# Half of the up product by Strassen's method in a fused retention and feed-forward kernel

## The chip, the cores and the metric

The kernel runs on one core of one Trainium2 chip. The metric is device microseconds (us) of one execution. Four compute engines work side by side, each strictly in the order of its own instructions: PE (matrix products, with its weight loads), DVE (VectorE), ACT (ScalarE) and POOL (GpSimd). SP issues most of the transfers. Engines wait for each other through semaphores.

## The reference

```python
scores = scale * np.matmul(q, k.transpose(0, 1, 3, 2))          # B=8 batches, H=8 heads, S=576, D=64
Dmat = np.where(rel >= 0, gamma[:, None, None] ** rel[None, :, :], 0.0)
ret = scores * Dmat[None, :, :, :]
attn = np.matmul(ret, v)
x = np.ascontiguousarray(attn.transpose(0, 2, 1, 3)).reshape(B * S, H * D)   # 4608 x 512
h = x @ w_in                                                     # 512 x 2048
g = h * np.clip(h + 3.0, 0.0, 6.0) / 6.0
out = g @ w_out                                                  # 2048 x 512
```

A decayed attention (retention) feeds a two-layer network. Its first product, `x @ w_in`, is the up product; the second, `g @ w_out`, is the down product.

## The kernel before

The 4608 tokens are taken in nine blocks of 512 (`NB = 9`). Block 0 holds the first 64 tokens of each batch, the other eight the remaining 512 of one batch each. Retention is worked in chunks of 128 tokens, four to a block, with a state carried from chunk to chunk.

Work is staged so that PE always has three kinds of it at hand. In stage `kb` of the last loop (L811 to L839) PE does the down product of block `kb`, the up product of block `kb+1`, and the retention of block `kb+2`. The order is written out by hand: `tc.manual_schedule` keeps each engine's instructions in the order in which the program issues them.

- **The up product** comes in 16 units per block (`up_steps`, L491). A unit is 128 rows of `h` by 512 tokens: four products over the four 128-row pieces of `d_model`. `product` (L149) splits each into two matmuls of 64 output rows. The result lies in a PSUM bank `ph`. ACT reads it, `u = relu(ph/6 + 0.5)` (L510); DVE finishes the gate, `g = min(u, 1) * ph` in fp16 (L512). `u` has three buffers.
- **The down product** from block 2 on is by Strassen's method (`down_strassen`, L562): seven products of 16 steps, 112 steps per block, each step two matmuls of 256 columns. I write D for a step. Its results lie in two banks `st`. ACT takes p1, p5, c11, c12 and u2 out of them (L595 to L631), DVE u3 and c21, and POOL adds in SBUF. The sums of quarters of `g` that it needs (s1 to s4, L517) are made on DVE by `side_sums` (L525), one at each "+" of the order.
- **Retention**, in letters of the order: c casts a chunk to fp16 (k on ACT, L188; q and v on POOL, L192 and L195), a scores, x and i the two halves of the output (`po`, copied to `xT` by ACT, L369), s the states, u the addition to the running state (DVE L313 and L316, then POOL L317), z its cast on ACT (L323 to L326).

The table `STEADY` (L710) gives after which unit each letter comes; `per = 7` puts seven D between two units. All PSUM tiles but those of the down product share six banks (tag "pp"), which are handed on in order. A unit that starts takes the bank that was taken six tiles earlier, once its last reader is done.

Of the kernel before, what the change touches and what calls it, by code (L numbers as in the profile page):

```python
# [21 lines left out]
def kernel(  # L22
# [9 lines left out]
    nc = tc.nc  # L32
# [3 lines left out]
    P = 128  # L36
# [39 lines left out]
    warm = const.tile([P, 1], FP32)  # L76
    mask = const.tile([P, P], FP16)
    SUB = P // 2
    query = const.tile([P, P], FP32)
    early = io.tile([P, H, D], FP32, tag="fv", name="early").rearrange("p h d -> p (h d)")  # L80
    dist, far = early[:, 0:P], early[:, P:2 * P]
# [5 lines left out]
    zh = [const.tile([P, NP, D], FP32, name=f"zh{b}") for b in range(B)]  # L87

    def indices():
        nc.vector.memset(half, 0.5)  # L90
# [58 lines left out]
    def product(out, lhs, rhs, **flags):  # L149

        for h2 in range(2):
            r = slice(h2 * D, h2 * D + D)
            nc.tensor.matmul(out[r], lhs[:, r], rhs, skip_group_check=True, **flags)  # L153
# [219 lines left out]


    def idle_products(n):
        idle = psum.tile([P, NP, P], FP32, tag="pp", name="idle")
        for _ in range(n):
            product(idle, ident16, ident16.unsqueeze(1).to_broadcast([P, NP, P]), start=True, stop=True)


    hd = {}
# [105 lines left out]
    def up_unit(kb, u, th=None):  # L487
        for _ in up_steps(kb, u, th):
            pass
# [39 lines left out]
    def store(kb, m2, o, m=slice(0, 2), cols=slice(0, DM)):  # L529
# [3 lines left out]
        else:  # L533
            rows = out.rearrange("(e m s) n -> e s m n", e=2, s=S)
            for e in range(2):
                nc.sync.dma_start(rows[e, 0:TL, 2 * m2:2 * m2 + 2, :], o[TL * e:TL * e + TL])

    def out_tile(kb, m2):
        return work.tile([P, 2, DM], FP32, tag=f"o{m2}", bufs=2, name=f"o{m2}_{kb}")

    kept = deque()


    def down_plain(kb):
# [139 lines left out]
    def do(todo):  # L684
        for what, c in todo:
            if what == "+":
                side_sums(c)
            elif c < NCH:
                {"c": cast, "t": lambda c: transposes(c, True, "kq" if c < PE_T else "k" if c < PE_K else ""), "a": scores, "s": states, "u": add, "z": past,
                 "x": cross_over, "i": inner, "k": keys_heads, "h": head_states, "o": lambda _: store(*kept.popleft())}[what](c)  # L690

    def go(plan, kb=None, down=None):
# [3 lines left out]
        for item in plan.split():  # L696
# [13 lines left out]
    STEADY = {0: [("u", 1)], 1: [("z", 1), ("+", 1)], 2: [("+", 1)], 4: [("c", 4)],  # L710
# [4 lines left out]

    FIRST_STEADY = {0: [("+", 1), ("c", 3)], 1: [("D", 7), ("a", 0), ("s", 0), ("u", 0)],
# [5 lines left out]

    with tc.manual_schedule(engines={ENG.PE, ENG.DVE, ENG.Pool, ENG.Activation, ENG.SP}):
        sp, act, pool = nc.sync, nc.scalar, nc.gpsimd
        on_act, on_dve = nc.scalar.copy, nc.vector.tensor_copy
        indices()
        for nm in ("k", "q"):
            landed = load_half(0, nm, 0, sp)
            keys = landed if nm == "k" else keys
            load_half(0, nm, 1, act)  # L730
        nc.scalar.activation(warm, half, ACTF.Exp)
        load_half(1, "q", 0, sp)
        load_half(1, "q", 1, act)
        for i in (2, 3):
            for e in range(2):
                load_half(i, "q", e, sp, keys)
        for i in (1, 2, 3):
            for e in range(2):
                load_half(i, "k", e, pool, None if i == 1 else keys)
            if i == 1:  # L740
                nc.gpsimd.memset(pick, 0.0)  # L741
        for i in range(NP):
            load_values(i)
        win_piece(0, 2)
        for n in (1, 2, 3):
            win_piece(n)
        wout = [wout_piece(pc) for pc in (0, 2, 1, 3)]
        distances()
        idle_products(5)
# [5 lines left out]
        idle_products(4)  # L755
# [9 lines left out]
        idle_products(1)  # L765
# [4 lines left out]
        idle_products(1)  # L770
# [37 lines left out]
        go("U1 D3 t14 U1 D2 U1 U1 D2 x13 a14 s14 i13 u14 z14 o1 c16 U1 D2 U1 D2 t15 U1 D2 U1 D2 +1 U1 x14 a15 s15 i14 u15 z15 "  # L808
           "c17 D2 U1 D2 +1 U1 D2 +1 U1 D2 x15 +1 U1 i15 t16 c18 +1 U1 D2 t17 U1 U1",
           2, down)  # L810
        for kb in range(2, NB):  # L811
            for _ in down:
                pass
            plain = kb < FIRST
            down = down_plain(kb) if plain else down_strassen(kb)
            per = 4 if plain else 7
            table = FIRST_STEADY if kb == 2 else STEADY
            c = NCB * (kb + 2)
            owed = 0
            for u in range(NFC):  # L820
                if u == 0:
                    owed += per - 2
                    for _ in range(per - 2):
# [5 lines left out]
                owed -= per  # L829
                while owed < 0:  # L830
                    next(down, None)
                    owed += 1
                for w, i in table.get(u, []):
                    if w == "D":
                        for _ in range(i):
                            next(down, None)
                        owed += i
                    else:
                        do([(w, i if w == "+" else c + i)])  # L839
        for _ in down:  # L840
            pass
# [30 lines left out]
```

## Time and profile before

| | |
|---|---|
| median of three runs | 300.67 us (300.67 to 300.8) |
| the profiled execution | 301.02 us, of which the profile's span is 299.3 us |
| PE busy | 287.4 us, 96% of the span |
| DVE, ACT, POOL busy | 216.2, 193.9, 133.7 us |
| stages kb = 2 to 7 in the span | 109.8 to 281 us, about 29 us each, the last 26 |
| clock of PE granted | 1.00 in every stretch |

A line of the timeline gives the start from the span's beginning, the time to the end, engine, line, operation, output and inputs, and how many instructions are merged. A bracket at its end gives idle time before it and what ended that. A line of the groups gives line, engine, operation, shapes and count, then busy time and the mean of one in ns, then idle time ahead of them. A line of the table by stretch gives, for each engine in the order PE, PEld (its weight loads), DVE, ACT and POOL, the busy time and the number of instructions.

### The profile page before, as it was taken

How to read it: one execution, taken by the hardware profiler on the slowest of the kernel's cores; microseconds unless marked ns; L12 is line 12 of the kernel's file. 1: busy time of each engine (PE TensorE's matmuls, PEld its weight loads, DVE VectorE, ACT ScalarE, POOL GpSimd, SP SyncE). 2: the span in 40 equal slices, each digit the busy share in tenths (PEclk: the TensorE clock that was granted, in tenths of full speed). 3: DMA queues.
4: the chain of work that ended last, by engine and by line, in shares of the span. 5: the costliest groups of instructions: out<-in, count | busy, mean ns of one | idle time of the engine just before them, and what ended most of it. 6: DMA issues, size and time to landing. Idle time of an engine off the chain costs nothing.

```text
span 299.3 us, 12661 instructions
## 1 busy us (share of the span) xinstructions
PE 287.4 (96%) x5574; PEld 219.3 (73%) x5574; DVE 216.2 (72%) x388; ACT 193.9 (65%) x360; POOL 133.7 (45%) x170
## 2 busy tenths in 40 slices
PE   4999998999999999999999999999999999999995
PEld 2776644777556667888777878778778987778894
DVE  7749545669897778788967797688869776647654
ACT  3748854799866696686677577667766574565420
POOL 8971057526762920719631962386247003100510
PEclk9999999999999999999999999999999999999999
DMA  6999999998999999997999999999906100200114
GB/s 157 157 182 213 186 227 209 227 228 183 161 216 164 249 202 191 178 239 195 225 220 225 169 201 216 150 177 247 148 3 142 72 2 30 102 15 2 72 72 140
DMA packets 119542, 47.86 MB, mean 160 GB/s; under 512 B 92352, under 2 KB 114880, under 8 KB 119488
## 3 DMA queue, kind: packets, MB, share of 16 engines
q1 hardware_dynamic: 114336, 41.56, 71.1%
q0 software_dynamic: 4720, 5.11, 10.5%
q8 instruction: 43, 0.70, 1.0%
q10 hardware_dynamic: 432, 0.39, 0.5%
q14 instruction: 11, 0.09, 0.1%
HBM read 36.70 MB, written 9.44 MB: 154 GB/s over the span
## 4 chain that ended last, share of the span: by engine, by line
PE 79%; DMA 9%; POOL 6%; SPq 2%; ACT 2%; issue 1%; DVE 1%; POOLq 0%; ACTq 0%
PE ph L153 37%; PE pm L153 29%; DMA wout<-in_moe_w_out_dram 6%; PE pd L153 5%; PE po L231 4%; DMA fq<-in_q_dram 2%; PE pa L231 2%; SPq L174 2%; POOL hv L439 1%; POOL hk L399 1%; POOL win L658 1%; PE pu L231 1%; POOL ws L741 1%; PE ptk L153 1%; POOL q L192 1%
## 5 line engine op out<-in xcount | busy, mean ns | idle before, releaser
L153 PE MATMUL ph<-xT,win 128*64 128x512 f16 (+1 forms) x1248 | 144.8, 364 | 1.2 <-DMA win<-in_moe_w_in_dram 0.5
L512 DVE SCALAR_TENSOR_TENSOR g<-u,ph 128x512 f16<-128x512 f32 (+1 forms) x156 | 98.8, 643 | 53.1 <-ACT u L510 52.6
L510 ACT ACTIVATE u<-ph,half 128x512 f32<-128x512 f32 (+1 forms) x156 | 100.5, 659 | 43.0 <-PE ph L153 40.6
L153 PEld LDWEIGHTS <-win 128*64 128x64 f16 x1248 | 82.9, 136 | 28.6 <-DMA win<-in_moe_w_in_dram 1.1
L153 PEld LDWEIGHTS <-g 128*64 128x64 f16 x928 | 51.1, 110 | 14.9 <-issue 0.4
L153 PEld LDWEIGHTS <-s 128*64 128x64 f16 x896 | 50.3, 110 | 8.1 <-issue 0.2
L317 POOL TENSOR_TENSOR z<-z,gpow 128x256 f32<-128x256 f32 x24 | 15.8, 657 | 69.1 <-DVE z L316 51.2
L153 PE MATMUL pm<-ws,s 128*64 128x256 f16 x672 | 45.6, 273 | 0.0
L192 POOL TENSOR_TENSOR q<-fq,dec 128x512 f16<-128x512 f32 x32 | 36.7, 1166 | 3.4 <-DVE zh L282 1.7
L369 ACT CAST xT<-po 128x256 f16<-128x256 f32 (+1 forms) x44 | 22.5, 583 | 23.4 <-PE po L231 22.5
L195 POOL TENSOR_TENSOR v<-fv,dec 128x512 f16<-128x512 f32 x32 | 35.4, 1111 | 2.1 <-DMA fv<-in_v_dram 2.1
L591 POOL TENSOR_TENSOR u<-u,p 128x512 f32<-128x512 f32 x7 | 8.9, 1271 | 60.4 <-ACT u L631 54.2
L153 PE MATMUL pd<-wout,g 128*64 128x512 f16 x256 | 34.7, 382 | 0.1
L153 PE MATMUL pm<-wout,g 128*64 128x256 f16 x448 | 31.1, 273 | 0.0
L266 DVE TENSOR_TENSOR a<-pa,mask 128x256 f16<-128x256 f32 (+1 forms) x44 | 21.9, 539 | 8.4 <-PE pa L231 4.7
L188 ACT CAST k<-fk 128x512 f16<-128x512 f32 x32 | 19.9, 622 | 2.1 <-DMA fk<-in_k_dram 2.1
L527 DVE TENSOR_TENSOR s<-g 128x1024 f16<-128x1024 f16 x28 | 19.3, 692 | 0.2
L323 ACT CAST z<-z 128x512 f16<-128x512 f32 x24 | 14.9, 622 | 5.1 <-DVE z L313 4.7
L153 PE MATMUL pm<-ws,g 128*64 128x256 f16 x224 | 16.7, 274 | 0.0
L153 PE MATMUL pm<-wout,s 128*64 128x256 f16 x224 | 16.3, 273 | 0.1
L527 DVE TENSOR_TENSOR s<-g,s 128x1024 f16<-128x1024 f16 x14 | 13.3, 949 | 0.0
L231 PE MATMUL po<-qT,z 64*64 64x64 f16 x512 | 12.5, 198 | 0.4 <-ACT z L326 0.3
(106 smaller groups left out, 270.0 us busy)
## 6 DMA issues: line engine op xcount, KB each, us to landing
fk<-in_k_dram SPq DMA_DIRECT2D x32, 256.0 KB, 4.6
fq<-in_q_dram SPq DMA_DIRECT2D x16, 512.0 KB, 6.0
fv<-in_v_dram SPq DMA_DIRECT2D x32, 256.0 KB, 5.5
out_dram<-o SPq DMA_DIRECT2D x14, 512.0 KB, 3.8
wout<-in_moe_w_out_dram POOLq DMA_DIRECT2D x4, 512.0 KB, 17.9
out_dram<-o SPq DMA_DIRECT2D x7, 256.0 KB, 5.4
win<-in_moe_w_in_dram POOLq DMA_DIRECT2D x3, 512.0 KB, 10.9
hq<-in_q_dram SPq DMA_DIRECT2D x6, 128.0 KB, 4.6
```

What stands on the lines that cost most here:

```text
L153: nc.tensor.matmul(out[r], lhs[:, r], rhs, skip_group_check=True, **flags)
L188: nc.scalar.copy(by_head(k16), in_rows(st[c]["fk"]))
L192: nc.gpsimd.tensor_tensor(by_head(q16[:, e]), in_rows(st[c]["fq"][:, :, e, :]), in_rows(dd[:, 2 + e, 0:H, :]), ALU.mult)
L195: nc.gpsimd.tensor_tensor(v16, st[c]["fv"], dd[:, 1, H:2 * H, :], ALU.mult)
L231: return lambda: nc.tensor.matmul(*args, skip_group_check=True, **flags)
L266: nc.vector.tensor_tensor(a16[:, a, 0:n].rearrange("p x i q -> p (x i) q"), pa[a].rearrange("p x i q -> p (x i) q"), m, ALU.mult)
L317: nc.gpsimd.tensor_tensor(new, new, decay, ALU.mult)
L323: nc.scalar.copy(z16, zs[c])
L369: nc.scalar.copy(xt[:, s], po[s].rearrange("p x n (e r) -> p x n e r", e=2))
L510: nc.scalar.activation(uu[:, 0:n], ph[:, 0:n], ACTF.Relu, bias=half, scale=1.0 / 6.0)
L512: nc.vector.scalar_tensor_tensor(out=g[:, hf, ths, jr, :], in0=by_half(uu), scalar=1.0, in1=by_half(ph), op0=ALU.min, op1=ALU.mult)
L527: nc.vector.tensor_tensor(*pend.popleft())
```

## The change

Stages 3 to 7 no longer follow `STEADY` but a new order, `PLAN`. In it eight of the 16 units, those of the first half of `d_ff`, are replaced by two groups of four, `up_quad`, called Q (its first part) and q (each later part). A group computes its 512 rows by 512 tokens in seven products of half the size instead of eight. Each of the seven is four product steps of 256 columns, which add up in three banks x, z and y. Partial results p and q are copied by ACT to SBUF, added by DVE or POOL, and gated as before. One of the four gates of a group is done by POOL in two instructions (`min`, then a product), the others by DVE.

The order inside a group, with names used later: x1 and z (product steps on PE), copy pa (ACT, bank x), z+=p (DVE); y1, copy q (ACT, bank y), gate z, x2, copy pb (ACT, bank x); y2, y+=p (DVE); x3, copy pc (ACT, bank x), gate y, q+=p (POOL); gate q (POOL); x4, gate x.

The method needs sums of quarters of `w_in` (made once by POOL, W) and of x (made for each block by two instructions on DVE, t1 and t2, and two on POOL, t3 and t4, at T). They take the room of tiles that are no longer used; the output tiles go from two buffers to one. At the start, idle products that keep PE occupied are 80 columns wide instead of 512, with more of them.

```diff
+    def sums_of_w(jq):
+        w, (s1, s2, s3, s4) = w_of(jq), [w_sums[jq][:, n] for n in range(4)]
+        a11, a12, a21, a22 = [w[:, 2 * k:2 * k + 2, JP * i:JP * i + JP] for i in range(2) for k in range(2)]
+        for o, x, y, op in ((s1, a21, a22, ALU.add), (s2, s1, a11, ALU.subtract), (s3, a11, a21, ALU.subtract),
+                            (s4, a12, s2, ALU.subtract)):
+            for c in range(2):
+                nc.gpsimd.tensor_tensor(o[:, c], x[:, c], y[:, c], op)
+    def sums_of_x(kb):
+        b11, b12, b21, b22 = [xts[kb][:, 2 * k:2 * k + 2, HB * t:HB * t + HB] for k in range(2) for t in range(2)]
+        t1, t2, t3, t4 = [x_sums[:, n] for n in range(4)]
+        nc.vector.tensor_tensor(t1, b12, b11, ALU.subtract)
+        nc.vector.tensor_tensor(t2, b22, t1, ALU.subtract)
+        nc.gpsimd.tensor_tensor(t3, b22, b12, ALU.subtract)
+        nc.gpsimd.tensor_tensor(t4, b21, t2, ALU.subtract)
+    def gate(kb, g, src, eng):
+        u = work.tile([P, BLK], FP32, tag="u", bufs=3, name=f"u{kb}")
+        u = u.rearrange("p (j t) -> p j t", j=JP)
+        nc.scalar.activation(u, src, ACTF.Relu, bias=half, scale=1.0 / 6.0)
+        if eng is nc.vector:
+            eng.scalar_tensor_tensor(out=g, in0=u, scalar=1.0, in1=src, op0=ALU.min, op1=ALU.mult)
+        else:
+            eng.tensor_scalar(u, u, 1.0, None, ALU.min)
+            eng.tensor_tensor(g, u, src, ALU.mult)
+    def up_quad(kb, jq):
...
+        def one(n, lhs, rhs, more=False):
+            for j in range(JP):
+                for c in range(2):
+                    product(b[n][:, j, :], lhs(c, j), rhs(c), start=(c == 0 and j == 0 and not more), stop=(c == 1))
+        b["x"] = bank("x")
+        one("x", plain(0, 0), x(0, 0))
+        nc.scalar.copy(p, b["x"])
+        b["z"] = bank("z")
+        one("z", plain(0, 1), x(1, 0))
+        nc.vector.tensor_tensor(b["z"], b["z"], p, ALU.add)
+        yield
+        b["y"] = bank("y")
+        one("y", summed(1), xs(1))
+        nc.scalar.copy(q, b["y"])
+        gate(kb, g[:, 0, 0:JP], b["z"], nc.vector)
+        one("x", summed(2), xs(2), True)
+        nc.scalar.copy(p, b["x"])
+        yield
+        one("y", summed(4), x(1, 1), True)
+        nc.vector.tensor_tensor(b["y"], b["y"], p, ALU.add)
+        yield
+        one("x", summed(3), xs(3), True)
+        nc.scalar.copy(p, b["x"])
+        gate(kb, g[:, 1, 0:JP], b["y"], nc.vector)
+        nc.gpsimd.tensor_tensor(q, q, p, ALU.add)
+        yield
+        gate(kb, g[:, 1, JP:JQ], q, nc.gpsimd)
+        yield
+        one("x", plain(1, 1), xs(4), True)
+        gate(kb, g[:, 0, JP:JQ], b["x"], nc.vector)
+        yield
-    STEADY = {0: [("u", 1)], 1: [("z", 1), ("+", 1)], 2: [("+", 1)], 4: [("c", 4)],
...
+    PLAN = ("D5 Q0 u1 c4 D4 q z1 +1 D6 q +1 D4 q D8 q D2 q U4 D7 U5 D13 a2 x0 s2 i0 u2 "
+            "U6 u3 +1 W1 c5 U7 D7 z2 +1 Q1 c6 z3 D4 q +1 D6 q D4 q +1 D8 q D2 q U12 D9 U13 D15 a4 x2 s4 i2 u4 D1 "
+            "U14 z4 c7 +1 U15 T D7 +1")
...
+            if SIDE <= kb < NB - 1:
+                steady(kb, down)
+                continue
```

`SIDE` is 3. `steady` walks through `PLAN`; W1 acts in stage 3 alone (W0 stands in stage 2). Casts (c) and most of retention run out with the chunks: stages 3, 4 and 5 have all of it, stage 6 has one group of scores and no casts, stage 7 has neither.

More of the change, by code (lines that the diff above doesn't have):

```diff
@@ L86 @@
     gpow = const.tile([P, NP], FP32)
-    zh = [const.tile([P, NP, D], FP32, name=f"zh{b}") for b in range(B)]
+    states_of_heads = const.tile([P, B, NP, D], FP32)
+    zh = [states_of_heads[:, b] for b in range(B)]
     def indices():
@@ L375, in idle_products @@
     def idle_products(n):
-        idle = psum.tile([P, NP, P], FP32, tag="pp", name="idle")
+        idle = psum.tile([P, 80], FP32, tag="pp", name="idle")
         for _ in range(n):
-            product(idle, ident16, ident16.unsqueeze(1).to_broadcast([P, NP, P]), start=True, stop=True)
+            product(idle, ident16, ident16[:, 0:80], start=True, stop=True)
     hd = {}
@@ L536, in store @@
                 nc.sync.dma_start(rows[e, 0:TL, 2 * m2:2 * m2 + 2, :], o[TL * e:TL * e + TL])
+    late_out = [const.tile([P, 2, DM], FP32, name=f"late{m2}") for m2 in range(2)]
     def out_tile(kb, m2):
-        return work.tile([P, 2, DM], FP32, tag=f"o{m2}", bufs=2, name=f"o{m2}_{kb}")
+        return late_out[m2] if kb == 1 else work.tile([P, 2, DM], FP32, tag=f"o{m2}", bufs=1, name=f"o{m2}_{kb}")
     kept = deque()
+    SIDE = 3
+    JP = JQ // 2
+    w_sums = {0: wout16[:, 0:JH, HM:DM].rearrange("p (n c) (j x) -> p n c j x", n=4, j=JP),
+              1: late_out[1].rearrange("p m n -> p (m n)").bitcast(FP16).rearrange(
+                  "p (n c j x) -> p n c j x", n=4, c=2, j=JP)}
@@ new lines, with w_of @@
+    x_sums = late_out[0].rearrange("p m n -> p (m n)").bitcast(FP16).rearrange("p (n c t) -> p n c t", n=4, c=2)
+    part = [const.tile([P, JP, HB], FP32, name="part0"),
+            states_of_heads[:, 0:2].rearrange("p b i d -> p (b i d)").rearrange("p (j t) -> p j t", j=JP)]
+    def w_of(jq):
+        return win16[jq].rearrange("p c (x j) -> p c j x", j=JQ)
+    def sums_of_w(jq):
[5 more added lines that the diff above has]
+                nc.gpsimd.tensor_tensor(o[:, c], x[:, c], y[:, c], op)
@@ new lines, in up_quad @@
+    def up_quad(kb, jq):
+        if (kb, jq) not in gt:
+            gt[kb, jq] = [gp.tile([P, 2, 2, JQ, HB], FP16, tag="g", bufs=4, name=f"g{kb}_{jq}")]
+        g = gt[kb, jq][0][:, 0]
+        w = w_of(jq)
+        plain = lambda i, k: (lambda c, j: w[:, 2 * k + c, JP * i + j, :])
+        summed = lambda n: (lambda c, j: w_sums[jq][:, n - 1, c, j, :])
+        x = lambda k, t: (lambda c: xts[kb][:, 2 * k + c, HB * t:HB * t + HB])
+        xs = lambda n: (lambda c: x_sums[:, n - 1, c, :])
+        bank = lambda n: psum.tile([P, JP, HB], FP32, tag="pp", name=f"pq{kb}_{jq}_{n}")
+        p, q = part
+        b = {}
+        def one(n, lhs, rhs, more=False):
[29 more added lines that the diff above has]
+        yield
@@ L748 @@
         distances()
-        idle_products(5)
+        idle_products(30)
         mask_of_heads(0)
@@ L754 @@
         mask_of_heads(1)
-        idle_products(4)
+        idle_products(23)
         cast_heads(0, "q", on_dve)
@@ L764 @@
         mask_of_heads(3)
-        idle_products(1)
+        idle_products(6)
         turn_heads(2, "k", on_act)
@@ L769 @@
         scores_heads(1)
-        idle_products(1)
+        idle_products(6)
         turn_heads(3, "k", on_act)
@@ L810, with steady @@
            2, down)
+        def steady(kb, down):
+            c0 = NCB * (kb + 2)
+            u, quad = 0, None
+            for item in PLAN.split():
+                what, n = item[0], int(item[1:] or 0)
+                if what == "D":
+                    for _ in range(n):
+                        next(down, None)
+                elif what == "U":
+                    up_unit(kb + 1, n)
+                elif what == "Q":
+                    quad = up_quad(kb + 1, n)
+                    next(quad)
+                elif what == "q":
+                    next(quad)
+                elif what == "T":
+                    if kb + 2 < NB:
+                        sums_of_x(kb + 2)
+                elif what == "W":
+                    if kb == SIDE:
+                        sums_of_w(n)
+                else:
+                    do([(what, n if what == "+" else c0 + n)])
         for kb in range(2, NB):
@@ L813 @@
                 pass
[L814 to L817, printed above, removed]
+            down = down_strassen(kb)
+            if SIDE <= kb < NB - 1:
+                steady(kb, down)
+                continue
+            table = FIRST_STEADY if kb == 2 else {}
             c = NCB * (kb + 2)
@@ L821 @@
                 if u == 0:
-                    owed += per - 2
-                    for _ in range(per - 2):
+                    owed += 5
+                    for _ in range(5):
                         next(down, None)
@@ L828 @@
                     side_sums(1)
[L829 removed]
+                owed -= 7
                 while owed < 0:
@@ L837 @@
                         owed += i
+                    elif w == "W":
+                        sums_of_w(i)
+                    elif w == "T":
+                        sums_of_x(kb + 2)
                     else:
```

3 lines of the change are left out of this document (1 added, 2 removed), and 8 rows, old and new, of tables (FIRST_STEADY, STEADY).

## The prediction

> **What bounds the kernel now.** I read the busy times first, then the stages one by one, then the chain that ended last, then each engine's timeline at a stage border.
>
> ```profile
> PE 287.4 (96%) x5574; PEld 219.3 (73%) x5574; DVE 216.2 (72%) x388; ACT 193.9 (65%) x360; POOL 133.7 (45%) x170
> ```
>
> The table by stretch, for one stage (kb = 4):
>
> ```profile
> 168.00:197.20 29.20, 29.20 (x606) 23.34 (x604) 22.54 (x39) 19.83 (x35) 15.17 (x15) 1.00 1.14 184
> ```
>
> PE is busy for all of it, DVE for 22.5 us, ACT for 19.8, POOL for 15.2. The chain gives PE's pace:
>
> ```profile
> 168.11 1.73 PE ph L153 x16
> 169.84 1.31 PE pm L153 x24
> 171.15 0.86 PE ph L153 x8
> ```
>
> A unit takes 0.86 us, and 24 matmuls of 256 columns (12 D) take 1.31, so a D takes 0.109. The twelve D are the last seven of block 3 and five of block 4. So the border is at 169.84 + 7 x 0.109 = 170.60, which I call t = 0. The other engines there:
>
> ```profile
> 169.32 0.70 ACT L510 ACTIVATE u<-ph,half 128x512 f32<-128x512 f32 x1
> ...
> 171.02 0.70 ACT L510 ACTIVATE u<-ph,half 128x512 f32<-128x512 f32 x1
> ```
> ```profile
> 170.66 0.94 DVE L527 TENSOR_TENSOR s<-g,s 128x1024 f16<-128x1024 f16 x1
> 171.75 0.69 DVE L512 SCALAR_TENSOR_TENSOR g<-u,ph 128x512 f16<-128x512 f32 x1
> 172.47 0.69 DVE L527 TENSOR_TENSOR s<-g 128x1024 f16<-128x1024 f16 x1
> 173.08 0.68 DVE L591 TENSOR_TENSOR o<-pm,u 128x512 f32<-128x512 f32 x1
> 173.68 0.68 DVE L512 SCALAR_TENSOR_TENSOR g<-u,ph 128x512 f16<-128x512 f32 x1
> ```
> ```profile
> 171.01 1.49 POOL L195 TENSOR_TENSOR v<-fv,dec 128x512 f16<-128x512 f32 x1
> 175.29 0.61 POOL L317 TENSOR_TENSOR z<-z,gpow 128x256 f32<-128x256 f32 x1 [2.79 <-DVE z L316]
> 175.87 2.94 POOL L192 TENSOR_TENSOR q<-fq,dec 128x512 f16<-128x512 f32 x2
> 178.77 1.04 POOL L195 TENSOR_TENSOR v<-fv,dec 128x512 f16<-128x512 f32 x1
> ```
>
> Here is what matters: at the border DVE and ACT are behind PE. Unit 15 left PE before 169.84; its gate on DVE starts at 171.75. PE does not feel it, since six banks lie between. When an engine has work queued it starts the next instruction about 0.6 us after the last (172.47, 173.08, 173.68); a dependent one waits for the whole 0.69, then starts within 0.05.
>
> **What the change takes from PE.** Four units take 4 x 0.865 = 3.46 us. A group has seven products of four pairs of 256 columns, 7 x 4 x 0.109 = 3.03. Gain 0.43 a group, 0.86 a stage, 4.3 us over five stages. Nothing else is gained.
>
> **What it adds.** From these groups:
>
> ```profile
> L595 ACT COPY p<-pm 128x512 f32<-128x512 f32 x7 | 4.1, 579 | 2.1 <-PE pm L153 2.1
> L591 DVE TENSOR_TENSOR u<-pm,p 128x512 f32<-128x512 f32 x6 | 4.1, 685 | 0.1
> L591 POOL TENSOR_TENSOR u<-u,p 128x512 f32<-128x512 f32 x7 | 8.9, 1271 | 60.4 <-ACT u L631 54.2
> ```
>
> Per group: four copies on ACT at 0.58, one instruction more on DVE at 0.69 (two sums, one gate less), and three on POOL: q+=p at 1.27, the fp16 product between 1.04 (a quiet cast of v) and 1.49, and `min`, which the trace does not show, between 0.20 (the small L123 on 4 elements) and 1.27. I take 0.8, nearer to the 0.61 of L317, which reads as many elements. Per stage t1 and t2 take about 0.33 each on DVE (half of the 0.69 of a sum of 1024; at most 0.69), t3 and t4 1.04 each (0.61 to 1.49). By sums all have room: ACT 24.5, DVE 24.6, POOL about 24 in a stage of 28.3. But the group turns slack into **waits**: x2, x3 and x4 add into the bank that ACT has to have copied, so PE now stands behind ACT and DVE several times in one group, where before it had six banks of distance. So I follow the queues. The order and the waits are those of the changed program as built; durations and backlog are those above.
>
> **First group, t from the border.** DVE: gate of unit 15 at 1.15, t1 1.75, t2 2.10 to 2.43, s1 2.42, c21 3.03, z+=p 3.63 to 4.31 (pa has been ready since 1.75). ACT: pa 1.17 to 1.75, cast of k, q to 3.36, then gate z's relu waits for z+=p: 4.34 to 5.03, then pb to 5.5. PE without waits: D5, x1 and z, D4 to 1.84, y1, x2, D6, y2, D4, and x3 at 4.21. With them: y1 waits for t1 until 2.15 (0.31 lost), x3 would start at 4.52 and waits for pb until 5.55 (**1.03** lost). Then DVE does gate z, s2, y+=p to 7.06, ACT pc to 7.67; x4, which would start at 7.07 (x3 0.43, ten D 1.09), waits until 7.72 (**0.65**). Together 2.0 us. In stage 7 neither casts nor additions of states lie in between, and the trace of its border (unit 15's gate on DVE 0.63 after it) gives 0.8 + 0.54 = 1.34.
>
> In stages 3, 4 and 5 POOL comes late as well. Its queue is: v of a chunk to 1.9, t3, t4 to 4.0, then the state's product (waits for DVE, 5.15), two casts of q (2.94 before, 2.04 elsewhere; 2.4 taken), v, and only then, at 9.2, q+=p, for which pc was ready at 7.7. q+=p ends at 10.5. Behind it in ACT's queue stand gate q's relu, gate x, unit 8 and p5: 10.55 + 3 x 0.6 + 0.55 = 12.9. PE has the 13th D after unit 9 at 11.95 and needs p5: **1.0** lost.
>
> **Second group.** By the same walk x2 and y2 wait 0.05 and 0.45 (casts and state casts ahead of pa and q on ACT), x3 0.15, x4 0.5 (gate z, s1 and y+=p on DVE between pb and pc). Then the firmest of all. Let pc end at T. PE: x4 0.43, unit 12 0.86, eight D 0.87: at T + 2.2 it needs u2 out of its bank, for the first D of the seventh product. ACT's queue behind pc: gate y, then gate q, which waits for q+=p until T + 1.35, gate x, unit 12, u2: 1.4 + 3 x 0.6 + 0.57 = T + 3.8. **1.6** lost in each of five stages, whatever the rest. Together 2.75 with retention, 2.05 in stages 6 and 7 (x4 and u2).
>
> Stage 3 has W1 too: eight instructions on POOL (0.61 each, from L317; 0.3 to 0.75) between the state's product at 17.2 and 22.1. y2 needs the last: 1.95 more. The casts behind it push q+=p to 26.6, and u2 comes 3.65 after its D instead of 1.6; without x3's and x4's waits, 3.35 more in all.
>
> **Sum.** Lost less 0.86 gained: stages 4 and 5 2.0 + 1.0 + 2.75 - 0.86 = 4.9 each, stage 3 4.9 + 3.35 = 8.25, stage 6 2.0 + 2.05 - 0.86 = 3.2, stage 7 1.34 + 2.05 - 0.86 = 2.5. 9.8 + 8.25 + 3.2 + 2.5 = 23.7. On the profiled execution's 301.02 (span 299.3) that is 324.7; it lies 0.35 above the median of the runs, so **324.4** against 300.67.
>
> **At nothing I cost** W0 in stage 2 (POOL is busy 11.6 of 29.2 us there; without that room about 5), the single output buffers (a store lands in 3.8 us, the next use is a stage later), and the idle products: 30 of 80 columns are 2400, five of 512 are 2560, and PE waits there for casts anyway (up to 0.8 later if each took a D's 0.109).
>
> **GpSimd and VectorE.** The two casts of q took 2.94 us while DVE made sums of g from SBUF, and 2.04 at 165.69, when DVE read PSUM; DVE's sum took 0.94 beside POOL's work and 0.68 in the quiet last stages. The Trainium skill, "SBUF — State Buffer", section "SBUF: two separate sides", says that a VectorE instruction with two inputs in SBUF and a GpSimd one that reads SBUF share a port pair that one holds for its whole length. The trace agrees, and the rule speaks against this change, which adds work on both sides of it. By the rows q+=p would then take 1.27 x 2.94 / 2.04 = 1.83; that is a rival below.
>
> **Rivals.** (1) POOL is in time: the casts of q pass in the gaps, W1 goes unseen. Then only the waits between PE, ACT and DVE stay: 3.2 in each of four stages, 2.5 in the last, +15.3: 316.0. For it: POOL idles half of the time now. Against: the order of its queue. (2) POOL and DVE block each other more: 0.56 more at each q+=p, 0.25 at each DVE sum on the path, about 1.4 in three stages and 0.8 in two, +5.8: 330. For it the 0.94 and 2.94; against, that q+=p has no DVE sum beside it for most of its length. (3) **Faster.** The place is u2 behind pc. A stage gains once u2 ends within 2.2 + 0.86 = 3.1 us of pc instead of 3.8, so if q+=p took under 0.6 instead of 1.27 and no other wait were left. With all hidden it gives -4.3, 296.4; with small remainders about 298. For it: the room in the sums of busy time. Against: 1.27 is measured for this very shape, and DVE's queue at the border stands in the trace. (4) The change does what it says and the two cancel, 300 to 301; or they leave a few us, 302 to 309.
>
> **Chances.** Forecast (319 to 328) 0.50, rival 1 (309 to 319) 0.26, rival 2 (328 to 336) 0.14, rival 3 (296 to 300) 0.06, rival 4 0.04, half of it without a difference. A measurement of this kernel can tell about 0.2% from no change. So faster 0.06, same 0.02, slower 0.92. Range 309 to 331: forecast, rival 1, and half of rival 2; W1's and `min`'s bounds move the sum by about 2 within it.
>
> **What would show it.** Right: in stages 3 to 7 PE has idle time ahead of the third and last products into bank x, and of the D after unit 12, ended by ACT's copies, some 3.4 us in stage 7 and 5.5 to 9 in stages 3 to 5; ACT's relu of gate q waits for POOL about 0.7 us or more; stages last 28.5 (stage 7) to 37 us. Wrong: PE busy throughout and stages 0.9 shorter (rival 3); POOL's q+=p starting right behind pc everywhere (rival 1); POOL's sums at 1.8 (rival 2).

## The result and the profile after

The changed kernel takes **347.04 us** (median of four runs, 345.53 to 347.54) against 300.67 before: ratio 1.155 (95% interval 1.150 to 1.160). The profiled execution took 346.77 us, its span 344.9, with a mean granted TensorE clock of 0.975. The forecast had the sign, but only half of the loss: 23.7 us against 45.8 by the profiled executions, and the time lies above the range.

The first line of each profile page, engine by engine, now reads:

```profile
PE 298.1 (86%) x5922; PEld 235.4 (68%) x5922; DVE 234.0 (68%) x408; ACT 213.1 (62%) x400; POOL 202.6 (59%) x226
```

PE was busy for 96% and is busy for 86%. The stretch of one stage (kb = 4, columns as in the line shown of before) says the same more sharply, and the last stage with groups (kb = 7) beside it shows the loss at its purest:

```profile
186.00:224.93 38.93, 32.27 (x649) 26.42 (x651) 25.55 (x41) 22.97 (x42) 25.42 (x22) 0.91 0.65 137
...
299.27:328.80 29.53, 26.24 (x405) 23.08 (x403) 18.66 (x32) 17.08 (x30) 13.38 (x11) 1.00 0.07 26
```

None of the engines that PE waits for is near its limit: DVE has 25.6 us of work in 38.9, POOL 25.4. The granted clock in stage 4 is 0.91, where it was 1.00.

Stage lengths from border to border (us). "Idle" is the idle time on PE in the changed kernel that the profile shows, "half" the time in which the clock was granted at half speed. A stage runs from the first D of its block to that of the next; in the kernel before, stages 2 to 7 lie from 111.36 to 283.21 us of the span, some 2 us behind the times of the first table. An idle time ahead of the first D of a block counts in the stage that it ends, here and below:

| stage | before | after | more | forecast more | idle | half |
|---|---|---|---|---|---|---|
| 2 | 29.85 | 29.95 | 0.1 | 0 | 0.1 | 0 |
| 3 | 29.23 | 45.67 | 16.4 | 8.25 | 12.0 | 6.8 |
| 4 | 29.03 | 38.93 | 9.9 | 4.9 | 6.7 | 6.8 |
| 5 | 29.20 | 39.36 | 10.2 | 4.9 | 8.1 | 3.4 |
| 6 | 28.51 | 34.99 | 6.5 | 3.2 | 5.9 | 0 |
| 7 | 26.04 | 29.52 | 3.5 | 2.5 | 3.3 | 0 |

Now where PE stands. This is its timeline in stage 4, with the other engines' links between; the bracket gives the idle time ahead of a row and what ended it:

```profile
188.97 0.63 PE L153 MATMUL pq_x<-late,wout 128*64 128x256 f16 x8 [0.49 <-DVE late L569]
...
191.98 0.63 PE L153 MATMUL pq_x<-late,wout 128*64 128x256 f16 x8 [0.85 <-ACT part L614]
...
194.15 0.66 PE L153 MATMUL pq_x<-late,win 128*64 128x256 f16 x8 [0.46 <-ACT part L620]
...
196.13 1.27 POOL L622 TENSOR_TENSOR states_of_heads<-states_of_heads,part 128x512 f32<-128x512 f32 x1
...
197.43 0.72 ACT L576 ACTIVATE u<-states_of_heads,half 128x512 f32<-128x512 f32 x1 [2.74 <-POOL states_of_heads L622]
...
198.24 1.49 POOL L580 TENSOR_SCALAR u<-u 128x512 f32<-128x512 f32 x1 [0.84 <-ACT u L576]
...
199.81 1.27 POOL L581 TENSOR_TENSOR g<-u,states_of_heads 128x512 f16<-128x512 f32 x1
199.83 0.30 PE L153 MATMUL pm<-wout,s 128*64 128x256 f16 x2 [1.22 <-ACT p L711]
...
201.11 0.69 ACT L510 ACTIVATE u<-ph,half 128x512 f32<-128x512 f32 x1 [1.33 <-POOL g L581]
...
201.83 0.69 DVE L512 SCALAR_TENSOR_TENSOR g<-u,ph 128x512 f16<-128x512 f32 x1 [1.78 <-ACT u L510]
...
202.57 0.48 PE L231 MATMUL pu<-v,k 64*64 64x64 f16 x18 [1.89 <-DVE g L512]
...
203.73 3.63 PE L153 MATMUL ph<-xT,win 128*64 128x512 f16 x16
```

Read it from the top. Product x3 waits for pb (L614) 0.85 us, x4 for pc (L620) 0.46, the next D for p5 (L711) 1.22: three of the forecast's waits, near their sizes (1.03, 0.65, 1.0); the section on the forecast compares them as the forecast counted. The one below them the forecast does not have. POOL's gate (`min`, L580, and product, L581) frees its u tile only at 201.1; unit 9's relu on ACT waits for that tile 1.33 us, its gate on DVE for the relu, and the states' product pu on PE for the gate's bank, **1.89 us**. Behind it 16 matmuls of 512 columns take 3.63 us; eight took 0.86 in the kernel before, so this is half the clock.

### The profile page after: what moved, and what is told of

Its sections match the earlier page's. It is cut to its first block, busy times and chain, and to the rows that moved or that the text cites. A ratio compares the mean times of both kernels' runs of the same rounds, so it can differ in the third digit from the quotient of the medians.

```text
span 344.9 us, 13482 instructions
## 1 busy us (share of the span) xinstructions
PE 298.1 (86%) x5922; PEld 235.4 (68%) x5922; DVE 234.0 (68%) x408; ACT 213.1 (62%) x400; POOL 202.6 (59%) x226
## 4 chain that ended last, share of the span: by engine, by line
PE 32%; POOL 24%; issue 17%; DVE 10%; DMA 8%; ACT 6%; SPq 2%; POOLq 0%; DVEq 0%; ACTq 0%
PE ph L153 12%; PE pm L153 10%; DMA wout<-in_moe_w_out_dram 5%; POOL q L192 5%; PE pd L153 4%; POOL states_of_heads L622 3%; POOL v L195 3%; DVE s L527 3%; PE po L231 2%; ACT u L510 2%; DVE g L512 2%; POOL wout L563 2%; POOL u L580 2%; SPq L174 2%; DMA fq<-in_q_dram 2%
## 5 line engine op out<-in xcount | busy, mean ns | idle before, releaser
L153 PE MATMUL ph<-xT,win 128*64 128x512 f16 (+1 forms) x928 | 107.9, 371 | 0.7 <-ACT xT L369 0.4
L512 DVE SCALAR_TENSOR_TENSOR g<-u,ph 128x512 f16<-128x512 f32 (+1 forms) x116 | 71.1, 629 | 47.7 <-ACT u L510 47.0
L153 PEld LDWEIGHTS <-win 128*64 128x64 f16 x1168 | 77.1, 138 | 29.4 <-issue 7.7
L510 ACT ACTIVATE u<-ph,half 128x512 f32<-128x512 f32 (+1 forms) x116 | 72.5, 650 | 29.0 <-PE ph L153 15.1
L622 POOL TENSOR_TENSOR states_of_heads<-states_of_heads,part 128x512 f32<-128x512 f32 x10 | 13.2, 1316 | 30.3 <-ACT part L620 30.3
L527 DVE TENSOR_TENSOR s<-g 128x1024 f16<-128x1024 f16 x28 | 24.6, 880 | 0.1
L580 POOL TENSOR_SCALAR u<-u 128x512 f32<-128x512 f32 x10 | 14.9, 1488 | 8.4 <-ACT u L576 8.4
L578 DVE SCALAR_TENSOR_TENSOR g<-u,pq_x 128x512 f16<-128x512 f32 x10 | 6.9, 688 | 18.6 <-ACT u L576 18.6
L576 ACT ACTIVATE u<-states_of_heads,half 128x512 f32<-128x512 f32 x10 | 7.2, 722 | 15.7 <-POOL states_of_heads L622 15.7
L153 PEld LDWEIGHTS <-wout 128*64 128x64 f16 x160 | 7.9, 109 | 12.4 <-ACT part L614 5.9
```

The lines of the kernel that those rows point to most:

```text
L510: nc.scalar.activation(uu[:, 0:n], ph[:, 0:n], ACTF.Relu, bias=half, scale=1.0 / 6.0)
L512: nc.vector.scalar_tensor_tensor(out=g[:, hf, ths, jr, :], in0=by_half(uu), scalar=1.0, in1=by_half(ph), op0=ALU.min, op1=ALU.mult)
L527: nc.vector.tensor_tensor(*pend.popleft())
L580: eng.tensor_scalar(u, u, 1.0, None, ALU.min)
L622: nc.gpsimd.tensor_tensor(q, q, p, ALU.add)
```

## The experiments

Times and stage lengths in us, together ahead of the single runs:

| run | time | ratio (95%) | stage 3 | 4 | 5 | 6 | 7 |
|---|---|---|---|---|---|---|---|
| after | 347.04 | 1.155 (1.150–1.160) | 45.67 | 38.93 | 39.36 | 34.99 | 29.52 |
| fill | 345.73 | 1.147 (1.131–1.163) | 45.85 | 38.46 | 38.30 | 34.98 | 29.53 |
| own_u | 339.70 | 1.127 (1.115–1.139) | 44.03 | 37.17 | 36.94 | 33.55 | 28.97 |
| sums_on_dve | 337.40 | 1.120 (1.108–1.131) | 40.39 | 36.62 | 37.00 | 34.56 | 29.49 |
| no_w | 340.47 | 1.130 (1.118–1.142) | 38.66 | 39.36 | 38.70 | 34.98 | 29.53 |
| after_old_idle | 346.22 | 1.148 (1.143–1.153) | 42.67 | 40.24 | 39.60 | 34.79 | 29.50 |
| apart | 323.02 | 1.078 (1.071–1.085) | 31.85 | 35.68 | 35.02 | 33.32 | 26.39 |
| light_only | 309.05 | 1.030 (1.025–1.035) | 30.95 | 29.02 | 31.30 | 33.18 | 26.39 |
| light_old_idle | 308.06 | 1.021 (1.017–1.026) | 29.76 | 30.05 | 31.09 | 33.20 | 26.39 |
| light_late_sums | 305.14 | 1.013 (1.009–1.017) | 29.44 | 29.36 | 29.57 | 31.74 | 27.29 |
| light_early_sums | 305.28 | 1.015 (1.011–1.019) | 28.98 | 29.16 | 29.02 | 31.57 | 27.82 |
| idle_only | 305.12 | 1.017 (1.013–1.022) | 31.99 | 29.03 | 29.68 | 28.48 | 26.04 |
| idle_8_columns | 304.25 | 1.009 (1.006–1.013) | 31.48 | 29.02 | 29.69 | 28.48 | 26.04 |

The kernel before, run on the same chips, had medians of 300.25 to 301.51, so a time here is read by its ratio.

**Is it the clock?** e1_fill puts idle products into the wait ahead of pu.

```diff
+    FILL = (20, 24, 28)
...
+        if c0 in FILL:
+            for _ in range(9):
+                product(gs[c0]["po"][0]..., ident16, ident16..., start=True, stop=True)
```

> The changed kernel with nine idle products (128 x 512 columns, 0.216 us each, 1.9 us in all) put between the first scores and the crossing products of stages 3, 4 and 5, where the profile after shows PE idle for 1.9 us ahead of the states' products. Every wait of the change stays. Theory A (what the forecast lacked is TensorE's clock, which halves after a stretch with too much idle time): the 1.9 us are filled, the half-clock stretches at 160.6, 201.5 and 242.5 of the trace after (3.4, 6.8 and 3.4 us) go, and the time falls by 5 to 7 us from 347 to 340 to 342. Rival B (the clock falls for another reason, or the half-clock stretches cost nothing since PE waits there anyway): the clock falls as before, and the time stays within 1.5 us or grows by up to 2.

The half clock in stages 4 and 5, 10.2 us of it, went away, and the two stages became only 0.5 and 1.1 us shorter. The clock went theory A's way, the time rival B's. What the faster clock won came back as waits: in stage 4 the second group's x3 now stands 0.87 us for pb, where it had not stood, and y1 and x2 stand 0.44 and 0.66 for t1 and t2, where x2 alone had stood 0.49; x3 and x4 of the first group stand as before. So here the half clock is mostly a follower of the waits. Stage 3, filled too, is as long as it was; its half clock came at other places, 10.2 us of it instead of 6.8.

**Is it POOL's u tile?** e2_own_u gives POOL's gate a tile of its own.

```diff
-        u = work.tile([P, BLK], FP32, tag="u", bufs=3, name=f"u{kb}")
+        if eng is nc.vector:
+            u = work.tile([P, BLK], FP32, tag="u", bufs=3, name=f"u{kb}")
+        else:
+            u = states_of_heads[:, 2:4].rearrange("p b i d -> p (b i d)")
```

> The changed kernel, with a buffer of its own for the u that GpSimd works on, so that unit 9's relu on ACT no longer waits for GpSimd's gate to hand a u buffer back. Theory A (chain of waits: GpSimd's gate, unit 9's relu, its gate on DVE, the bank of the states' products): PE's 1.9 us of idle time ahead of the states' products in stages 3 to 5 fall to 0.6 to 0.9, stage 6's 1.4 to about 0.5; four or five us in all, and 2 to 7 us more if half-clock stretches go with them: 336 to 343. Rival C (GpSimd's own pace and its shared port with DVE hold the stage, not this buffer): the idle time moves to another wait of the same stage, and the time stays within 2 us of 347.

339.70, 7.3 us less. PE's line in the table of waits, first of after and then of own_u (us in total, times, longest):

```profile
PE pu L231 <- DVE g L512: 7.1, 4, 1.9
```
```profile
PE pu L231 <- DVE g L512: 1.4, 3, 0.5
```

The gap is gone but for 0.46 a stage, which is the unit's own relu and gate. So the wait was the tile's, and with it went at least the time that it had cost: the idle time ahead of pu fell by 5.7 us.

**POOL's part as a whole.** e3_sums_on_dve moves q+=p and the fourth gate to DVE.

```diff
-        nc.gpsimd.tensor_tensor(q, q, p, ALU.add)
+        nc.vector.tensor_tensor(q, q, p, ALU.add)
-        gate(kb, g[:, 1, JP:JQ], q, nc.gpsimd)
+        gate(kb, g[:, 1, JP:JQ], q, nc.vector)
```

> The changed kernel with GpSimd taken out of the groups: q+=p and the gate of q are done by DVE. Theory A: in the first group q+=p no longer stands behind GpSimd's casts, p5's wait (1.22 us in stages 3 to 5) goes, the states' wait (1.9) falls below 0.7, and most half-clock stretches go; in the second group q+=p now stands behind gate y on DVE, so u2's wait grows from 1.35 to about 2 us. In all 333 to 338. Rival C (DVE is the engine that is short, GpSimd relieves it): DVE's longer queue delays z+=p and y+=p in both groups by 0.6 us or more, and the time is 347 or more.

337.40, 9.6 us less, with DVE doing more. The wait for p5 fell from 1.22 to 0.54, that of pu from 1.89 to 0.47, and the one for u2 rose from 1.35 to 1.91: q+=p now stands behind gate y on DVE and ends 1.92 us behind pc instead of 1.35 (stage 4). A gate on DVE is one instruction of 0.69; on POOL it is 1.49 + 1.27.

**The sums of w_in.** e4_no_w leaves out the sums of w_in (W0 and W1 do nothing, and the groups read old values).

```diff
+    w_sums[1] = w_sums[0]
...
     def sums_of_w(jq):
+        return
```

> The changed kernel without the sixteen sums of w_in on GpSimd (it reads other data of the same shape in their place, so a part of the computation is left out). Theory A: stage 2 no longer holds back the store of block 1's output, so the 1.46 and 0.56 us of PE's idle time at the first group of stage 3 (t1 and t2 wait for that store) go, and u2's wait of 3.3 us in stage 3 falls to 1.35, the second half-clock stretch (177.6) goes: stage 3 shrinks from 45.7 to about 39, the others stay, 340 to 341. Rival D (the sums cost nothing, stage 3 is long because its casts and loads come late): stage 3 stays over 44.

340.47; all of it in stage 3, 45.67 to 38.66. So the sums cost 7.0 us, with the 3.4 us of half clock that went with them: W1's part was forecast with 3.35, W0's with nothing. The run does not split the two. The chain that ended last shows how W0 costs, though W0 runs from 12 to 5 us before the border of stage 3:

```profile
128.45 6.65 POOL wout L563 x8
135.10 1.68 POOL u L678
...
136.85 1.28 POOL o L678
...
138.15 0.40 SPq L532
...
138.60 4.32 DMA out_dram<-late
142.92 0.02 issue
142.94 0.72 DVE late L568
```

W0 holds POOL for 6.65 us; behind it POOL's additions that finish an output tile end at 138.1; SP sends that tile first, and after it the one in whose room the sums of x are to lie. That store lands at 142.9, and only then may t1 start. PE stands for it at the top of stage 3:

```profile
143.80 0.63 PE L153 MATMUL pq_y<-late,wout 128*64 128x256 f16 x8 [1.46 <-DVE late L568]
144.99 0.63 PE L153 MATMUL pq_x<-late,wout 128*64 128x256 f16 x8 [0.56 <-DVE late L569]
```

In no_w y1 does not wait and x2 waits 0.67.

**All waits taken apart.** e5_apart starts with block 5 (`SIDE = 4`), gives the partial results three buffers and POOL's gate the third of them, puts the POOL gate behind the other three and t1 to t4 ahead of the border.

```diff
-    SIDE = 3
+    SIDE = 4
...
+        gate(kb, g[:, 1, JP:JQ], q, nc.gpsimd, p3)
...
-    PLAN = ("D5 Q0 u1 c4 D4 q z1 +1 D6 q +1 D4 q D8 q D2 q U4 D7 U5 D13 a2 x0 s2 i0 u2 "
+    PLAN = ("D5 U4 D7 u1 c4 U5 z1 +1 D4 Q0 D4 q +1 D6 q D4 q D10 q U6 D9 a2 x0 s2 i0 u2 q u3 U7 +1 c5 D7 z2 +1 "
+            "Q1 c6 z3 D4 q +1 D6 q D4 q +1 D11 q U12 q D8 U13 D15 a4 x2 s4 i2 T u4 D1 U14 z4 c7 +1 U15 D7 +1")
```

> A version of the change in which PE no longer stands directly behind ACT and DVE: the groups start after two plain units of a stage instead of at its border, the partial copy pc has a buffer of its own, each copy stands ahead of the relu that it stood behind, q's gate comes after another unit, u2 is copied before x4, the sums of x are made before units 14 and 15, and the groups start in stage 4, with the sums of w_in in stages 2 and 3. Theory A (the loss is made of these waits, and the halved clock follows from them): PE's idle time falls from 3.3 to 8.1 us to below 1.5 us a stage in stages 4 to 7, no half-clock stretch is left, each of these stages comes within 1.5 us of its length before (29.0, 29.2, 28.5, 26.0), and the time is 297 to 304. Rival E (DVE and ACT have too little time for seven partial results, in whatever order): stages 4 and 5 stay over 32 us, with PE waiting for DVE's or ACT's queue at other places, and the time is over 308.

323.02: 24 us less than after, but far from 297 to 304, on rival E's side. p5's wait and u2's are gone; a new one stands at the four borders behind stages 3 to 6, 1.6 to 2.4 us, and is the largest of all. DVE around the border of stage 4 in apart, and PE there:

```profile
171.00 1.26 DVE L569 TENSOR_TENSOR late<-xT,late 128x512 f16<-128x512 f16 x1
172.19 0.41 DVE L313 TENSOR_TENSOR z<-pu,states_of_heads 128x256 f32<-128x256 f32 x1
172.70 0.42 DVE L316 TENSOR_TENSOR z<-pu,z 128x256 f32<-128x256 f32 x1
173.04 0.68 DVE L679 TENSOR_TENSOR u<-pm,p 128x512 f32<-128x512 f32 x1
```
```profile
PE pm L153 <- DVE u L679: 8.5, 4, 2.4
```

The sum u3, which frees the bank for the next block's first D, stands behind t1 and t2. I had moved the sums of x out of the way of the groups and into the way of u3.

**Fewer stages.** e6_light_only is apart with groups in stages 6 and 7 alone, where POOL has least to do (`SIDE = 6`).

> The version before this one with the groups in stages 6 and 7 alone, where casts on GpSimd and ACT have run out; stages 3 to 5 as in the kernel before. Theory A: PE gains 0.86 us in each of the two stages and loses little: 298 to 301. Rival E: 302 or more, with idle time on PE in stages 6 and 7.

309.05, again on rival E's side. Stage 7 lasts 26.39, against 26.04 without groups; stage 6 33.18 against 28.51. Two other stages are longer by 1.7 and 2.1 without a group in them: stage 5 by the wait at its end (1.47) and a halt on PE that no semaphore ended (0.47), stage 3 by another such halt (1.79).

**The idle products.** e7_idle_only is the kernel before with the new idle products alone, 65 of 80 columns for 11 of 512. e9_idle_8_columns cuts them to 8 columns.

```diff
-            product(idle, ident16, ident16.unsqueeze(1).to_broadcast([P, NP, P]), start=True, stop=True)
+            product(idle, ident16, ident16[:, 0:80], start=True, stop=True)
...
-        idle_products(5)
+        idle_products(30)
```

> The kernel before with nothing of the change but its idle products at the start (65 of 80 columns in place of 11 of 512). Theory A: they lie beside waits for loads and casts, the time stays within 1 us of before, 299.7 to 301.7. Rival F: PE reaches stage 2 a microsecond earlier, as the trace after has it (first step of the down product by Strassen's method at 110.4 instead of 111.4 us), and the time falls by about 1 us.

> The kernel before with 65 idle products of 8 columns: as many instructions on PE as in idle_only, a tenth of its columns. Theory A (the number of instructions on PE decides where its stream halts): the gap of about 2 us at 155 us is there again, in the same matmuls of po, and the time is 304 to 306. Rival B (what counts is how long the idle products keep PE occupied, their columns): no gap, or a start that is longer by more than 1 us, and then another time: 300 to 302 without the gap, over 306.5 if the start suffers.

They cost 1.7% (305.12), which neither theory of idle_only had, and 0.9% with a tenth of the columns (304.25). Most of the loss of idle_only is not where the products are: it is one halt of about 2 us in stage 3 and two of 0.5. Here is the long one in idle_only, idle_8_columns and light_only; "issue" says that nothing the profile shows ended it.

```profile
155.65 0.21 PE L231 MATMUL po<-a,v 64*64 64x64 f16 x1 [2.05 <-issue]
```
```profile
157.73 0.21 PE L231 MATMUL po<-a,v 64*64 64x64 f16 x1 [1.77 <-issue]
```
```profile
155.31 0.21 PE L231 MATMUL po<-a,v 64*64 64x64 f16 x1 [1.79 <-issue]
```

It lies ahead of the last of 32 matmuls. The table by stretch, up to just before each halt, counts PE's matmuls in its brackets (first two kernels, then light_only):

```profile
0.00:155.60 155.60, 145.54 (x3035) 104.71 (x3035) 114.19 (x221) 109.23 (x217) 83.93 (x125) 1.00 1.04 202
```
```profile
0.00:157.70 157.70, 147.48 (x3035) 106.31 (x3035) 114.51 (x221) 109.07 (x217) 83.40 (x124) 1.00 1.04 199
```
```profile
0.00:155.25 155.25, 145.69 (x3035) 104.02 (x3035) 115.89 (x221) 109.07 (x217) 90.79 (x132) 1.00 1.03 198
```

It is matmul 3,036 in all three, at three different times. So the place hangs on the count of instructions, as theory A of idle_8_columns had it, not on columns or time. Its rival held in part as well: up to the border of stage 2 idle_8_columns took 113.71 us against 111.36 before, by the profiled executions. The second halt, of 0.43 to 0.50 us, lies in all three behind 4,568 matmuls. But apart, with the same 65 products, halts at matmul 3,036 too, and for 0.38 us only: the count fixes the place and not the length.

The traces also show what PE waits for. A queue of kind "instruction" brings packets of 16 KB, one for 128 to 130 of PE's matmuls with their weight loads in every kernel; here of before (5,574 matmuls) and of after (5,922):

```profile
q8 instruction: 43, 0.70, 1.0%
q8 instruction: 46, 0.75, 0.9%
```

The 14 traces hold 36 halts of PE over 0.07 us that nothing released. All of them lie ahead of a matmul whose number is 89 to 94 more than a multiple of 128, and all end 1.25 to 1.64 us after a packet of this queue has landed (1.35 to 1.37 for the long ones above). So PE stands there for its next stretch of instructions. No run shows why a packet comes in time at one of these places and 2 us late at another.

**The same undone in the changed kernel.** e8_after_old_idle and e10_light_old_idle put the old idle products back.

> The changed kernel with the idle products of the kernel before (11 of 512 columns instead of 65 of 80). Theory A: the 4.4 us that the narrow idle products cost in the kernel before came from one gap of 2.05 us and two of 0.5 on PE, ended by no semaphore, whose place depends on how many instructions PE has had; in the trace of after only one such gap of 0.61 us lies behind the start, so the time stays within 1.5 us of after, 345.5 to 348.5. Rival B: the narrow products cost the same in every kernel: 342 to 344.

> Groups in stages 6 and 7 alone, their waits taken apart (as in light_only), with the idle products of the kernel before. Theory A: light_only at 309.05 holds two parts, about 4.4 us of the idle products and about 4 us of waits in the groups' stages (gaps of 3.9 in stage 6 and 2.2 in stage 7, less a gain of 0.86 each): 304 to 306, with no gap at 155 us. Rival B: the gap at 155 us is not the idle products' but comes with any addition to the program: 308 to 310.

after_old_idle: 346.22, within the spread of after, so hardly anything of the 46 us is theirs; stage 3 is 3.0 shorter, stages 4 and 5 together 1.6 longer. light_old_idle: 308.06, 1.0 less than light_only (2.7 by the ratios, whose intervals overlap). The halt of 1.79 is gone, and others, 0.84 us of "issue" in stage 4 and 0.64 for a DMA, have come. So the time is rival B's and the vanished halt theory A's, and neither holds: an edit shifts the kernel against the places where packets are due, and the halts don't add up like terms.

**The sums of x once more.** e11_light_late_sums and e12_light_early_sums move t1 to t4 behind the border: behind the second unit of the stage, or behind its first.

```diff
-                    if kb + 2 < NB:
-                        sums_of_x(kb + 2)
+                    sums_of_x(kb + 1)
...
-    PLAN = ("D5 U4 D7 u1 c4 U5 z1 +1 D4 Q0 ... a4 x2 s4 i2 T u4 D1 U14 ..."
+    PLAN = ("D5 U4 D7 u1 c4 U5 z1 +1 T D4 Q0 ... a4 x2 s4 i2 u4 D1 U14 ..."    (late)
+    PLAN = ("D5 U4 T D7 u1 c4 U5 z1 +1 D4 Q0 ... a4 x2 s4 i2 u4 D1 U14 ..."    (early)
```

> As light_old_idle, but the sums of x (t1 to t4) are made 1 us after the border, behind the third unit's place, instead of ahead of it. Theory A: the waits of 1.47 and 1.59 us at the two borders of stages 6 and 7 (the sum u3 on DVE stood behind t1 and t2) go, with some 0.15 each for the restart: 3.0 to 3.5 us below light_old_idle, 300.5 to 303. Rival B: y1 then waits for t1 or t2 at the start of the group, 0.5 to 1.5 us in each stage, and the gain is 0.5 to 2: 302.5 to 305. Rival C, what the change was for: below 300.2, the first version that beats the kernel before.

> As light_late_sums, with t1 and t2 two units earlier, right behind the first unit of the stage. Theory A (what is left is the place of these two instructions in DVE's queue): the waits of y1 for t1, 1.65 us in stage 6 and 0.73 in stage 7, go with their restarts, 2.4 to 2.8 us below light_late_sums: 301.5 to 303.5, still not below the kernel before, since about 0.4 + 0.8 + 0.6 us of other waits stay and the gain of two stages is 1.7. Rival B: t1 and t2 then delay the gate or the sum that frees the next bank, and the wait appears there: 304 to 306. Rival C: the version beats the kernel before, below 300.

Both waits at the borders went, and 2.9 us with them (305.14). Then y1 waits for t1, 1.65 us in stage 6, as rival B had it. With t1 earlier that is gone too, and the next link is late, pa on ACT. PE in late_sums and in early_sums:

```profile
234.83 0.63 PE L153 MATMUL pq_y<-late,wout 128*64 128x256 f16 x8 [1.65 <-DVE late L568]
```
```profile
233.08 0.63 PE L153 MATMUL pq_x<-late,wout 128*64 128x256 f16 x8 [0.68 <-ACT part L605]
```

Stage 6 gains 0.2 by it, stage 7 loses 0.5, and the time is the same (305.28). Theory A of early_sums failed: a wait on this path is exchanged for the next. No version beat the kernel before; all of stage 6 is still 3.1 us longer than without groups, and the time saved on PE there is 0.86.

## Why the forecast was right in sign and wrong in size

- **The gain of 0.86 a stage and what bounds the kernel: nothing speaks against it.** All that follows is loss.
- **The waits on ACT's copies and u2: right in kind, and mostly in size.** Stage 7 has nothing else; these are its five gaps on PE:

```profile
304.44 0.63 PE L153 MATMUL pq_x<-late,wout 128*64 128x256 f16 x8 [0.74 <-ACT part L614]
306.57 0.66 PE L153 MATMUL pq_x<-late,win 128*64 128x256 f16 x8 [0.41 <-ACT part L620]
...
317.72 0.63 PE L153 MATMUL pq_x<-late,late 128*64 128x256 f16 x8 [0.38 <-ACT part L614]
319.85 0.66 PE L153 MATMUL pq_x<-late,win 128*64 128x256 f16 x8 [0.41 <-ACT part L620]
...
323.59 0.30 PE L153 MATMUL pm<-ws,s 128*64 128x256 f16 x2 [1.35 <-ACT u L718]
```

  They are 3.29 us of idle time, and the forecast named "some 3.4" of it as its sign. But its sum counts something else: how much later a matmul starts than in a dense stream. A matmul's row ends some 0.2 us after the next one could have started (two matmuls of 256 columns alone take 0.30, while in a dense stretch such a pair takes 0.11), so each gap costs about 0.21 more than its bracket: stage 7 lost 3.48 + 0.86 = 4.34 us. Counted in this way u2's "firmest" wait is 1.56, forecast 1.6, and x3 and x4 of the first group in stage 4 are 1.06 and 0.67, forecast 1.03 and 0.65. In stage 7 the sum had 1.34 + 2.05 = 3.39. The 0.95 that it lacks there are x3 of the second group (0.59, put at nothing in that stage), x4 behind it (0.62 for 0.45) and 0.23 at the first group. The wait of 0.45 at y2 of the second group did not come in stages 4 to 7.
- **POOL behind its queue: half right, and here the forecast failed first.** q+=p is late and p5 waits 1.22, 1.43 as counted above (forecast 1.0). But I followed POOL's gate no further than its relu. `min`, taken as 0.8 from the row with the like number of elements, takes 1.49; and the tile that it holds is one of three that the units' gates use. The groups of after:

```profile
L580 POOL TENSOR_SCALAR u<-u 128x512 f32<-128x512 f32 x10 | 14.9, 1488 | 8.4 <-ACT u L576 8.4
L622 POOL TENSOR_TENSOR states_of_heads<-states_of_heads,part 128x512 f32<-128x512 f32 x10 | 13.2, 1316 | 30.3 <-ACT part L620 30.3
L581 POOL TENSOR_TENSOR g<-u,states_of_heads 128x512 f16<-128x512 f32 x10 | 12.7, 1268 | 0.8
...
L569 DVE TENSOR_TENSOR late<-xT,late 128x512 f16<-128x512 f16 x5 | 5.3, 1069 | 0.2
```

  The missing wait, 1.89 us in three stages and 1.38 in a fourth, is the largest single error; own_u shows it at 7.3 us. L622 at 1.32 is the forecast's 1.27.
- **W0 "at nothing": wrong, and the clause on cover was nearer.** The forecast wrote that without room on POOL it costs about 5. It looked at POOL's idle time, not at what stands behind POOL: the output tile, the store order on SP, and the room that t1 writes. W0 and W1 together cost 7.0 (no_w) where 3.35 was counted. The other two terms at nothing held: the idle products are worth less than the spread in this kernel (after_old_idle), and the single output buffers brought PE no wait of their own (the one gap that the profile puts down to a store, 1.22 in stage 3, has the place and size of p5's).
- **t1 and t2 at 0.33 each: too low.** They took 0.61 and 1.07 on the mean. The bound given was 0.69. L569 at 1.26 runs beside POOL's L570 (1.34), and took 0.43 in early_sums with POOL between two sums. That fits the exchange between DVE and POOL that rival 2 feared, at other instructions than q+=p, which it priced at 1.83 and which did not grow (1.32); no run tried it alone.
- **The clock: not in the forecast.** 17.1 us of the five stages ran at half clock, at most 8.5 us of loss. fill shows that most of a stage's part is covered by the waits behind it.

The account of the stages: 46.46 us more where 23.75 were forecast, so 22.7 are missing. The forecast's waits were 28.05 (23.75 and the gain of 4.3). Counted as it counted, the 41 gaps cost 44.6 (36.0 idle, 0.21 more at each), 16.5 more. Of these the pu wait is 7.9 (7.06 idle and four restarts). The waits of y1 and x2 for t1 and t2 in stages 3 to 6 are 5.0 (6.2 for 1.24, in stage 3 with W0 behind them), those for p5 1.3. The other 6.2 of the 22.7 lie within the 8.5 that the half clock can cost at most; how much of it would have come as waits instead, the runs do not separate.

## What to carry to other kernels

A method that saves multiplications but adds into a bank which another engine has to have read turns an engine with six banks of slack into one that waits; follow each partial result through every queue until something else's buffer is free, and also through the tiles that it borrows (own_u: 7.3 us for one tile). Work moved to an engine with idle time is free only if nothing ordered behind it there is awaited: W0 in half-empty POOL held back a store, and the store a sum on DVE. And where a stream of short instructions runs without slack, count its instructions: 54 added products at the start, 80 or 8 columns wide, put a halt of 2 us elsewhere.

## What the runs showed of the hardware

**The clock fell to half without a long idle stretch.** The page's line of the granted clock, in 40 slices:

```profile
PEclk9999999999999999998989969999899999999999
```

The half-clock stretches began at 160.6, 177.6, 201.5 and 242.5 us and lasted 3.4 us or twice that; the distances between the starts are 5, 7 and 12 times 3.41. In the 3.41 us ahead of each, PE was idle for 1.9, 2.7, 2.0 and 2.3 us, in the last two cases in two gaps (1.22 and 1.89) with work between. The Trainium skill, "TensorE: Matmul & The Clock Gate", section "Part 1: The HAM clock gate (the "warmup" mystery)", gives a window of 3413 ns, running free of the kernel, and half rate after at least one idle window. The trace agrees with the window, and not with the condition: none of these was idle throughout. By the measurement, gaps of 1.2 to 1.9 us close together are enough. All starts within one trace lie whole multiples of 3.41 us apart, so each trace can be cut into such windows. In the seven kernels whose clock fell within the stages there are 20 falls from full clock, each behind a window with 1.59 to 2.74 us of idle time on PE; of the 588 other windows at full clock from 20 us on, 583 had 1.49 or less and none more than 1.91.

**One-input work on GpSimd was dearer than two-input work.** `min` on 128x512 took 1.49 us, the product of two such tiles 1.27, in all ten groups of the changed kernel.

**PE halted where its next packet of instructions was due.** The packets hold 16 KB and last for 128 to 130 matmuls. PE stood 1.8 to 2.1 us ahead of the same matmul of three programs, in a stretch where 32 matmuls pass within 0.5 us, and went on 1.35 to 1.37 us after the packet had landed.
